# Hash logits of 14 heads in two products per half, compared in PSUM, in a fused LSH attention and MoE kernel

## The chip, the cores and the metric

One NeuronCore of a Trainium2 chip runs the whole kernel in one launch. The metric is device time in microseconds (us); lower is better. Matrix products run on TensorE (PE in the profile, its weight loads PEld), elementwise work on VectorE (DVE), ScalarE (ACT) and GpSimd (POOL), and SyncE (SP) issues nearly all DMAs.

## What is computed

Three stages in a row, all in float32 at the interface:

```python
q_bits = (einsum('bhsd,dk->bhsk', q, proj) > 0)      # 2 batches, 8 heads, 768 tokens, 64 channels, 6 bits
k_bits = (einsum('bhsd,dk->bhsk', k, proj) > 0)
mask   = bucket(q_bits)[..., :, None] == bucket(k_bits)[..., None, :]
scores = where(mask, q @ k.T / 8, -1e9)
x      = softmax(scores) @ v                         # -> 1536 x 512
x      = gelu_sigmoid(x @ w_in) @ w_out              # 512 -> 2048 -> 512
x      = mish(x @ w2_in) @ w2_out                    # 512 -> 2048 -> 512
```

The products run in a reduced format (fp32r), so each operand is split into a high part (the rounded value) and a low part (the remainder), and a product is the sum of high x high, low x high and high x low.

## The kernel before, in words

Attention takes the first 230 us or so. Its 16 heads are 96 steps of 128 queries (`NSTEP`), six steps to a head. In a step, PE computes one block of scores (`qk`, line 613: two products of `kh` with `qx`, two of `kb` with `qb`, 384 columns each), transposes two blocks of earlier probabilities (`trp`, line 676, six products), and multiplies earlier probabilities with the values (`pv`, lines 700 and 701). DVE takes the row minimum while it moves the scores to SBUF (`clamp`, line 625), ACT takes the exponential (`expo`, line 638). The transposed blocks are rounded by ACT (`pth`, line 683) and their remainder is taken by DVE (`ptl`, line 688). The order of a step is a string, `ORDER = "ACaBbETQPR"`: A and B are the two transposes with ACT's rounding, C the clamp, a and b DVE's remainders, E the exponential, T whatever a table of due steps (`todo`) holds for this step, Q the scores of the next step, P and R the products with the values. Every engine and every DMA queue works strictly in the order in which this loop issues. Transposes work on groups of three steps: a step whose number is a multiple of three opens a group, and its first transposes need the exponential of the step just before.

A head's operands are prepared about one head ahead by `prep(n)`. For head n, with b = 6(n-2), GpSimd starts at step b+2 (`start_prep`, function `s0` and `s1`): it scales and rounds q (high q goes into `qk_m`, and a DMA moves it to the lower half of `qx`), makes low q, copies `kh` (k is stored twice, in both halves of the partitions) and makes low k in `qk_m`. At step b+8 `s2` computes the hash logits in PE, six products of 384 columns (for either half of the tokens: `qk_m`, `kh` and `qx` against the projection matrix `pwt`), into one PSUM bank `prep`; right behind it DVE compares with 0 and scales into mask rows `mk`. Four DMAs (`s5`) copy rows of `mk` into `qb` and `kb`, where they add a large penalty to the scores of unequal buckets; `s4` (step b+5) moves low k and high q into the other rows of `qb` and `kb`, and `s3` (step b+6) splits the values (`vv`). For head 2 the steps are fixed: start at step 5, logits at 8, mask DMAs at 9; head 3 starts at step 8. The scores of head n are first needed at Q of step b+11.

GpSimd also merges the heads' outputs (`x_out`, `x_split`), and near the end of attention makes operands of the first MoE stage: `x_ops` (lines 301 to 315, L109), the weight sums `sf` (`ssums`, lines 277 to 283) and a weight split (L261). ACT rounds the sums (`sh`, line 291) at step 89. Every one of these has its due step in `todo`. After attention the MoE stages run 500 us of products with PE never idle for long.

Of the kernel before, what the change touches and what calls it, by code (L numbers as in the profile page):

```python
# [30 lines left out]
def mask_consts():  # L31
    c = np.zeros((64, 2), np.float32)
    c[12:18, 0] = -3.0e38
    c[0:18, 1] = 1.0
    c[38:44, 0] = -3.0e38
    c[32:38, 1] = -2.0 * CBIG
    c[38:50, 1] = CBIG
    return np.concatenate([c, c])
# [3 lines left out]
def lsh_attention_moe_kernel(  # L42
# [10 lines left out]
    B, H, D, S = qt.shape  # L53
    NTOK, DM = out.shape
# [56 lines left out]
    def rnd(ap):  # L111
        return ap.bitcast(F32)
# [238 lines left out]
    def attention():  # L351
        with ExitStack() as es:
# [18 lines left out]
            def load_q(n):  # L371
                b, h = head(n)
                t = nat.tile([P, S], F32, tag="qn", name="qn")
                if n == 0:
                    for f in range(2):
                        c = slice(f * HS, (f + 1) * HS)
                        nc.sync.dma_start(t[0:D, c], qt[b, h, 0:D, c])
                else:
                    nc.sync.dma_start(t[0:D], qt[b, h])
                nat_t["q", n] = t  # L380
# [63 lines left out]
            def pcol(j, o):  # L444
                w = pw[:, j, o : o + 2 * NB * (2 if o else 1)]
                return w.rearrange("p (a b) -> p a b", a=2)[:, :, 0:NB]

            def prep_w():
# [6 lines left out]
                nc.scalar.mul(pcol(0, 0), rnd(pr), -1.0)  # L455

            opnd = {}

            def prep(n):
# [41 lines left out]
                def s2():  # L501
                    pt = ps_t.tile([P, 512], F32, tag="pt", name="prep")
                    logits(pt, 0, 64, True, False)
                    logits(pt, 1, 0, False, True)
                    mk_box.append(pt)
# [11 lines left out]
                def s4():  # L517
                    nc.sync.dma_start(rnd(qb[D:P]), rnd(qk_m[0:D]))
                    nc.sync.dma_start(rnd(kb[D:P]), rnd(qk_m[D:P]))

                def s5():
                    mk = mk_box.pop()
                    for f in range(2):
                        c = slice(f * HS, (f + 1) * HS)
                        rows = (qb, f * D), (kb, f * D + 32)
                        for t, r in rows[::-1] if f else rows:
                            nc.sync.dma_start(rnd(t[0:32, c]), mk[r : r + 32])
# [62 lines left out]
                return s0, s1, s2, s3, s4, s5  # L590
# [166 lines left out]
            todo = {}  # L757

# [7 lines left out]
            at(1, zero_rows)  # L766

# [53 lines left out]
            for i in range(NSTEP + PVLAG):  # L821
# [14 lines left out]
                for op in ORDER if i != 2 else ORDER.replace("TQ", "QT"):  # L836
# [402 lines left out]
def layouts(q, k, v, proj, moe_w_in, moe_w_out, moe2_w_in, moe2_w_out):  # L1239
# [3 lines left out]
    qt = q.transpose(0, 1, 3, 2)  # L1243
# [44 lines left out]
```

## Time and profile before

| | |
|---|---|
| device time, 3 runs | 734.85, 732.07, 731.7 us (median 732.07) |
| the profiled execution | 733.5 us, of which 731.7 us is the span of the trace |
| PE busy | 724.4 us (99% of the span), 3856 products |
| DVE, ACT, POOL busy | 615.7, 468.5, 185.4 us |
| the chain that ended last | PE 91%, DVE 3%, ACT 3% of the span |
| lines of the chain | MoE output products (947) 35%, scores (613) 9%, transposes (676) 8%, values (700, 701) 8%, hash logits (493) 2% |
| granted TensorE clock | 1.0 of full speed throughout (2.4 GHz) |

Busy shares are means over stages. Up to about 225 us (attention) GpSimd is busy most of the time and then never again; PE is busy all the time in both. A time in the rows below is from the start of the span; a bracket behind a row tells how long the engine sat idle before it and what ended the wait.

### The profile page before, as it was taken

Reading aid. Unit: us, or ns where it says so; the run is one execution under the profiler, and the core shown is the slowest. Engines: PE = TensorE matmul, PEld = TensorE weight load, DVE = VectorE, ACT = ScalarE, POOL = GpSimd, SP = SyncE. Lnnn points to the kernel's source line nnn. Section 1 sums busy time; section 2 is a strip of 40 time slices with the busy share of each in tenths; the row PEclk is TensorE's granted clock in tenths of the full one; section 3 lists DMA queues with packets and bytes.
Section 4 is the critical chain, followed back from the end, with each engine's and each line's share of the span. In section 5 each row is a group of like instructions: output and inputs, shape, how many; then the busy total and the mean of one; then the engine's idle time right before and its main releaser. Section 6 shows DMA issues by size and latency. Waiting matters only on the chain.

```text
span 731.7 us, 11140 instructions
## 1 busy us (share of the span) xinstructions
PE 724.4 (99%) x3856; PEld 631.5 (86%) x3856; DVE 615.7 (84%) x1134; ACT 468.5 (64%) x956; POOL 185.4 (25%) x188
## 2 busy tenths in 40 slices
PE   8999999999999999999999999999999999999998
PEld 5999999999998688888888888888888888888886
DVE  8888889989988859888878797998699899897864
ACT  7888888888898765536546465676635556455340
POOL 7958877878893000000000000000000000000000
PEclk9999999999999999999999999999999999999999
DMA  5745655656624311122211221301302222211004
GB/s 151 199 130 142 192 154 148 182 151 163 165 85 129 98 59 59 57 70 76 86 58 58 87 86 59 116 0 59 108 8 76 69 70 74 87 58 58 1 1 172
DMA packets 25992, 69.53 MB, mean 95 GB/s; under 512 B 4464, under 2 KB 6992, under 8 KB 25936
## 3 DMA queue, kind: packets, MB, share of 16 engines
q1 hardware_dynamic: 25632, 68.62, 31.9%
q8 instruction: 30, 0.49, 0.3%
q10 hardware_dynamic: 304, 0.20, 0.1%
q14 instruction: 26, 0.21, 0.1%
HBM read 49.09 MB, written 3.19 MB: 71 GB/s over the span
## 4 chain that ended last, share of the span: by engine, by line
PE 91%; DVE 3%; ACT 3%; DMA 1%; issue 1%; SPq 0%; POOL 0%; DVEq 0%; ACTq 0%
PE y L947 35%; PE X L1010 11%; PE s L613 9%; PE pt L676 8%; PE Y L1010 8%; PE W L1010 7%; PE u L701 4%; PE u L700 4%; PE h L346 2%; PE prep L493 2%; DMA rb<-scr 1%; ACT p L638 1%; ACT pth L683 1%; DVE wb L243 0%; DMA qn<-in_qt_dram 0%
## 5 line engine op out<-in xcount | busy, mean ns | idle before, releaser
L688 DVE TENSOR_TENSOR ptl<-pt,pth 128x384 fp32r<-128x384 f32 x192 | 98.1, 552 | 23.3 <-ACT pth L683 20.9
L683 ACT CAST pth<-pt 128x384 fp32r<-128x384 f32 x192 | 82.8, 484 | 29.6 <-PE pt L676 29.6
L638 ACT ACTIVATE p<-p,mn 128x768 f32<-128x768 f32 x96 | 91.2, 950 | 1.7 <-DVE p L625 1.4
L625 DVE TENSOR_SCALAR_CACHE_REDUCE p<-s 128x768 f32<-128x768 f32 x96 | 90.6, 945 | 1.1 <-PE s L613 1.1
L961 DVE TENSOR_TENSOR xq<-xq,y 128x512 f32<-128x512 f32 (+1 forms) x113 | 75.6, 679 | 13.8 <-PE y L947 13.0
L676 PE MATMUL pt<-ident,p 128*128 128x128 f32 x576 | 81.0, 274 | 0.1
L947 PE MATMUL y<-wh,gh 128*128 128x512 f32 (+1 forms) x194 | 75.4, 389 | 0.0
L947 PE MATMUL y<-wl,gh 128*128 128x512 f32 (+1 forms) x194 | 75.4, 389 | 0.0
L947 PE MATMUL y<-wh,gl 128*128 128x512 f32 (+1 forms) x194 | 75.2, 387 | 0.0
L947 PE MATMUL y<-gh,wh 128*128 128x512 f32 x192 | 75.1, 391 | 0.0
L947 PE MATMUL y<-gh,wl 128*128 128x512 f32 x192 | 74.9, 390 | 0.0
L947 PE MATMUL y<-gl,wh 128*128 128x512 f32 x192 | 74.7, 389 | 0.0
L259 ACT CAST wh<-wb 128x512 fp32r<-128x512 f32 x64 | 39.4, 619 | 54.6 <-DVE wb L246 26.2
L676 PEld LDWEIGHTS pt<-ident,p 128*128 128x128 f32 x576 | 68.5, 140 | 6.5 <-ACT p L638 2.4
L700 PE MATMUL u<-pth,vv 128*128 128x384 f32 x192 | 64.7, 337 | 0.0
L701 PE MATMUL u<-ptl,vv 128*128 128x384 f32 x192 | 64.5, 336 | 0.0
L613 PE MATMUL s<-kh,qx 128*128 128x384 f32 x192 | 55.6, 370 | 0.3 <-DVE p L625 0.3
L613 PE MATMUL s<-kb,qb 128*128 128x384 f32 x192 | 49.2, 337 | 1.1 <-POOL kb L109 0.9
L261 DVE TENSOR_TENSOR wl<-wb,wh 128x512 fp32r<-128x512 f32 x62 | 42.3, 687 | 3.9 <-ACT wh L259 3.6
L961 DVE TENSOR_TENSOR yr<-yr,y 128x512 f32<-128x512 f32 x56 | 38.2, 684 | 7.8 <-PE y L947 6.9
L947 PEld LDWEIGHTS y<-wh,gl 128*128 128x128 f32 x194 | 36.4, 188 | 7.6
L947 PEld LDWEIGHTS y<-gl,wh 128*128 128x128 f32 x192 | 36.0, 188 | 7.8
(271 smaller groups left out, 1841.6 us busy)
## 6 DMA issues: line engine op xcount, KB each, us to landing
raw<-in_wt_dram SPq DMA_DIRECT2D x64, 512.0 KB, 3.4
kn<-in_kt_dram SPq DMA_DIRECT2D x15, 384.0 KB, 5.0
vn<-in_vt_dram SPq DMA_DIRECT2D x8, 384.0 KB, 6.5
ul<-uh SPq DMA_DIRECT2D x16, 192.0 KB
rb<-scr SPq DMA_DIRECT2D x16, 192.0 KB, 3.6
qn<-in_qt_dram SPq DMA_DIRECT2D x15, 192.0 KB, 3.4
qx<-qk_m SPq DMA_DIRECT2D x15, 192.0 KB, 3.9
qb<-qk_m SPq DMA_DIRECT2D x15, 192.0 KB, 5.4
```

The lines of the kernel that those rows point to most:

```text
L261: sub(lo, wf, rnd(hi))
L613: nc.tensor.matmul(s[:, f, :HS], a[:, c], bb[:, f * HS : (f + 1) * HS], start=st, stop=not st,)
L625: nc.vector.tensor_scalar(sb, s[:, :, :HS], NEG, None, ALU.min, ALU.min, accum_out=mn)
L638: nc.scalar.activation(p, p, AF.Exp, bias=mn, scale=-1.0, accum_out=z_t[u][:, zc : zc + 1],)
L676: nc.tensor.transpose(ptile[:, j * P : (j + 1) * P], p_t[3 * g + j][:, t * P : (t + 1) * P], ident,)
L683: nc.scalar.copy(hi, ptile[:, :HS])
L688: nc.vector.tensor_sub(lo, ptile[:, :HS], rnd(hi))
L700: nc.tensor.matmul(ut[:, :HS], vv[:, t, :], hi, start=(t == 0), stop=False)
L701: nc.tensor.matmul(ut[:, :HS], vv[:, t, :], lo, start=False, stop=(t == NT - 1))
L947: nc.tensor.matmul(y, w[:, js] if m == 0 else x[:, js], x if m == 0 else w[:, i0:i1], start=(n == 0), stop=(n == 5),)
L961: nc.vector.tensor_add(acc, acc, y)
L1010: nc.tensor.matmul(bk[b], w[:, k], x, start=(first and i == 0), stop=(hook is not None and i == 2), skip_group_check=True,)
```

## The change

Heads 2 to 15 no longer use `pwt` with three operands but one 128-column matrix `px` with two operands, `qx` (low q above, high q below) and `qk_m` (high k above, low k below), so that a half takes two products, four in all. The high and the low products land in different rows of the PSUM bank: ACT copies the rows 64 to 127, negated, into `mk`, DVE compares the rows 0 to 63 with them (`is_gt`), and GpSimd multiplies the 32 rows that belong to `kb` by a constant. For this q is loaded twice, as k already was (128 partitions, 384 KB), GpSimd makes `kh` first and all of `qx` in one scaling, and the DMA that moved high q into `qx` is replaced by one (`s6`) that moves high k into `qk_m`. The steps are: start b+2, `s6` b+3, logits and ACT's copy b+7, compare and multiply at C of step b+8 (`mid`), mask DMAs at T of b+8. For head 2: start 5, `s6` 5, logits 8, compare 9, mask DMAs 9. `px` is filled once, at steps 1 and 4: a memset, three small copies and two small DMAs. The mask rows that are copied are 12 of 32.

```diff
     D //= 2
-                    nc.sync.dma_start(t[0:D], qt[b, h])
+                    nc.sync.dma_start(t, qt[b, h])
...
             def zero_rows():
...
+                nc.gpsimd.memset(rnd(px), 0.0)
...
+            def prep_x():
+                o = 32 + NB
+                q, k, ql, kl = (slice(x, x + 2 * NB) for x in (12, 44, 76, 108))
+                pcopy(px[:, 0, q], rnd(pw[:, 0, 0 : 2 * NB]))
+                pcopy(px[0:D, 1, k], rnd(pw[0:D, 1, o : o + 2 * NB]))
+                pcopy(px[D:P, 1, k], rnd(pw[D:P, 2, o : o + 2 * NB]))
+                nc.sync.dma_start(rnd(px[D:P, 0, ql]), rnd(pw[0:D, 2, 0 : 2 * NB]))
+                nc.sync.dma_start(rnd(px[0:D, 1, kl]), rnd(pw[D:P, 1, o : o + 2 * NB]))
...
                 def s0():
+                    if n > 1:
+                        pcopy(kh, kn)
+                        nc.gpsimd.tensor_scalar(qx, qn, QSCALE, 1.0, ALU.mult, ALU.mult)
+                        nc.gpsimd.tensor_scalar(qn[0:D], qn[0:D], QSCALE, 1.0, ALU.mult, ALU.mult)
+                        nc.gpsimd.tensor_sub(qx[0:D], qn[0:D], rnd(qx[0:D]))
+                        return
                     nc.gpsimd.tensor_scalar(qk_m[0:D], qn[0:D], QSCALE, 1.0, ALU.mult, ALU.mult)
                     nc.sync.dma_start(rnd(qx[D:P]), rnd(qk_m[0:D]))
-                    if n > 1:
-                        nc.gpsimd.tensor_scalar(qn[0:D], qn[0:D], QSCALE, 1.0, ALU.mult, ALU.mult)
-                        nc.gpsimd.tensor_sub(qx[0:D], qn[0:D], rnd(qk_m[0:D]))
 
                 def s1():
-                    pcopy(kh, kn)
                     nc.gpsimd.tensor_sub(qk_m[D:P], kn[D:P], rnd(kh[D:P]))
...
                 def s2():
                     pt = ps_t.tile([P, 512], F32, tag="pt", name="prep")
+                    mk_box.append(pt)
+                    if n > 1:
+                        for f in range(2):
+                            for j, x in enumerate((qx, qk_m)):
+                                nc.tensor.matmul(
+                                    pt[:, :HS],
+                                    px[:, j, 12 - 12 * f : 140 - 12 * f],
+                                    x[:, f * HS : (f + 1) * HS],
+                                    start=(f + j == 0),
+                                    stop=(f + j == 2),
+                                )
+                        mk = hd.tile([P, HS], F32, tag="mk", name="mk", bufs=1)
+                        mk_box.append(mk)
+                        nc.scalar.mul(mk[0:64], pt[64:128, :HS], -1.0)
+                        return
...
+                def s2m():
                     if n > 1:
-                        s2m()
-
-                def s2m():
+                        pt, mk = mk_box
+                        del mk_box[0]
+                        nc.vector.tensor_tensor(mk[0:64], pt[0:64, :HS], mk[0:64], ALU.is_gt)
+                        nc.gpsimd.tensor_scalar(
+                            mk[32:64], mk[32:64], -2.0 * CBIG, 1.0, ALU.mult, ALU.mult
+                        )
+                        return
...
                 def s4():
-                    nc.sync.dma_start(rnd(qb[D:P]), rnd(qk_m[0:D]))
+                    nc.sync.dma_start(rnd(qb[D:P]), rnd(qx[D:P] if n > 1 else qk_m[0:D]))
...
+                def s6():
+                    nc.sync.dma_start(rnd(qk_m[0:D]), rnd(kh[0:D]))
...
-                for f, early, late in ((s2, 8, 8), (s3, 11, 6), (s4, 6, 5), (s5, 9, 9)):
+                for f, early, late in ((s6, 5, 3), (s2, 8, 7), (s3, 11, 6), (s4, 6, 5), (s5, 9, 8)):
                     at(early if n == 2 else b0 + late, f)
+                mid.setdefault(9 if n == 2 else b0 + 8, []).append(s2m)
...
                     elif op == "C" and i < NSTEP:
                         clamp(i)
+                        for f in mid.pop(i, ()):
+                            f()
```

How the instructions move, at three places. Line numbers in the rows are those of the kernel that a row is from; a number behind a name tells tiles of one name apart.

First place, PE in the steady cycle, at the logits of head 4 (`prep` the logits, `s` scores, `pt` transposes of the probabilities `p`). Before:

```order
L493 MATMUL prep_895<-qx_666,pwt_146 128x384
L613 MATMUL s_904<-kh_446,qx_447 128x384 x2
L613 MATMUL s_904<-kb1_142,qb1_140 128x384 x2
...
L676 MATMUL pt_913<-ident_123,p_806 128x128
L676 MATMUL pt_913<-ident_123,p_840 128x128
L676 MATMUL pt_913<-ident_123,p_873 128x128
```

After:

```order
L524 MATMUL prep_863<-qk_m_683,px_149 128x384
L655 MATMUL s_870<-kh_453,qx_454 128x384 x2
L655 MATMUL s_870<-kb1_142,qb1_140 128x384 x2
...
L718 MATMUL pt_880<-ident_123,p_709 128x128
L718 MATMUL pt_880<-ident_123,p_743 128x128
L718 MATMUL pt_880<-ident_123,p_777 128x128
...
L655 MATMUL s_914<-kh_453,qx_454 128x384 x2
L655 MATMUL s_914<-kb1_142,qb1_140 128x384 x2
...
L718 MATMUL pt_923<-ident_123,p_813 128x128
L718 MATMUL pt_923<-ident_123,p_847 128x128
L718 MATMUL pt_923<-ident_123,p_887 128x128
```

Before, the transposes after the logits' step open a new group; now a whole step with the last transposes of the old group (p_709 to p_777) stands between them.

Second place, GpSimd and SP around head 2 (`kb1`, `qb1` are zeroed rows of head 1's operands, `vv` the values). GpSimd before:

```order
L109 TENSOR_SCALAR qb1_140<-zero_137 32x768
L473 TENSOR_SCALAR qk_m_338<-qn_212 64x768
L476 TENSOR_SCALAR qn_212<-qn_212 64x768
L477 TENSOR_TENSOR qx_337<-qn_212,qk_m_338 64x768
L109 TENSOR_SCALAR kh_336<-kn_214 128x768
L481 TENSOR_TENSOR qk_m_338<-kn_214,kh_336 64x768
...
L473 TENSOR_SCALAR qk_m_448<-qn_374 64x768
...
L481 TENSOR_TENSOR qk_m_448<-kn_376,kh_446 64x768
L109 TENSOR_SCALAR vv_563<-vn_444 128x6x64
```

After:

```order
L111 TENSOR_SCALAR qb1_140<-zero_137 32x768
L437 MEMSET px_149 128x280
L111 TENSOR_SCALAR px_149<-pwt_146 128x12
L111 TENSOR_SCALAR px_149<-pwt_146 64x12 x2
L111 TENSOR_SCALAR kh_343<-kn_215 128x768
L490 TENSOR_SCALAR qx_344<-qn_213 128x768
...
L111 TENSOR_SCALAR kh_453<-kn_383 128x768
...
L498 TENSOR_TENSOR qk_m_455<-kn_383,kh_453 64x768
L543 TENSOR_SCALAR mk_466<-mk_466 32x384
L111 TENSOR_SCALAR vv_570<-vn_451 128x6x64
```

The multiply of head 2's mask (mk_466) stands behind all of head 3's preparation (kh_453 to qk_m_455), and `px` ahead of head 2's. SP there, after:

```order
L569 DMA qb0_139<-mk_466 12x384
L569 DMA kb0_141<-mk_466 12x384
L569 DMA kb0_141<-mk_466 12x384
L569 DMA qb0_139<-mk_466 12x384
L559 DMA qk_m_455<-kh_453 64x768
```

Head 3's move of high k into `qk_m` stands behind the mask DMAs of head 2.

Third place, GpSimd near the end of attention (`z` row sums, `sf` weight sums, `t2h` to `b21h` operands of the first MoE stage). Before:

```order
L650 TENSOR_SCALAR z_2818<-z_2818 128x12
L313 TENSOR_TENSOR xq_74<-xq_74 128x512 x2
L279 TENSOR_TENSOR sf_3239<-wb_1892,wb_2786 128x256
L109 TENSOR_SCALAR t2h_3344<-xq_74 128x512
L301 TENSOR_TENSOR t2l_3345<-xq_74,t2h_3344 128x512
L281 TENSOR_TENSOR sf_3239<-sf_3239,wb_1892 128x256
L315 TENSOR_TENSOR xq_74<-xq_74 128x512
L109 TENSOR_SCALAR b21h_3389<-xq_74 128x512
L283 TENSOR_TENSOR sf_3239<-wb_1892,sf_3239 128x256
```

After:

```order
L692 TENSOR_SCALAR z_2825<-z_2825 128x12
L315 TENSOR_TENSOR xq_74<-xq_74 128x512 x2
L281 TENSOR_TENSOR sf_3246<-wb_1899,wb_2793 128x256
L543 TENSOR_SCALAR mk_3326<-mk_3326 32x384
L111 TENSOR_SCALAR t2h_3360<-xq_74 128x512
L303 TENSOR_TENSOR t2l_3361<-xq_74,t2h_3360 128x512
L283 TENSOR_TENSOR sf_3246<-sf_3246,wb_1899 128x256
L317 TENSOR_TENSOR xq_74<-xq_74 128x512
L111 TENSOR_SCALAR b21h_3400<-xq_74 128x512
L285 TENSOR_TENSOR sf_3246<-wb_1899,sf_3246 128x256
```

The multiply of head 15's mask (mk_3326) stands in the middle of this work, ahead of the last sums.

## Rows read from the trace of the kernel before

**Rows 1.** The chain of waits, 60 to 100 us: by line, then one piece

```profile
by line: PE s L613 31.3%; PE pt L676 30.7%; PE u L701 15.3%; PE u L700 14.8%; PE prep L493 7.8%; PE prep L657 0.5%
...
65.09 1.04 PE prep L493 x6
```

**Rows 2.** Timeline, PE: start us, us, engine line op tile, idle before

```profile
80.89 0.81 PE L676 MATMUL pt<-ident,p 128*128 128x128 f32 x6
...
87.03 1.03 PE L676 MATMUL pt<-ident,p 128*128 128x128 f32 x6
```

**Rows 3.** Waits, all engines: total us, times, longest

```profile
PEld pt L676 <- ACT p L638: 2.4, 10, 0.3
```

**Rows 4.** Timeline, ACT, ahead of the transposes at 87.03 us

```profile
86.31 0.95 ACT L638 ACTIVATE p<-p,mn 128x768 f32<-128x768 f32 x1
```

**Rows 5.** Timeline, POOL, then PE, at the start

```profile
8.11 1.29 POOL L109 TENSOR_SCALAR kb<-qk_m 64x384 fp32r<-64x384 f32 x1
9.45 0.79 PE L613 MATMUL s<-kb,qb 128*128 128x384 f32 x3 [0.91 <-POOL kb L109]
```

**Rows 6.** Windows: us, busy of PE PEld DVE ACT POOL, PEclk, DMA share, GB/s

```profile
5.00:6.00 1.00, 0.75 (x5) 0.65 (x4) 0.94 (x3) 0.95 (x3) 0.54 (x1) 1.00 0.99 255
...
7.00:8.00 1.00, 0.98 (x6) 0.54 (x5) 1.00 (x2) 0.51 (x1) 0.92 (x2) 1.00 0.86 338
```

**Rows 7.** Timeline, POOL, up to head 3's preparation

```profile
1.25 0.47 POOL L438 MEMSET wzero<- 128x448 f32 x1
...
3.68 0.20 POOL L109 TENSOR_SCALAR pwt<-pr 64x12 fp32r<-64x12 f32 x1
...
15.16 0.82 POOL L473 TENSOR_SCALAR qk_m<-qn 64x768 fp32r<-64x768 f32 x1
...
29.69 0.51 POOL L109 TENSOR_SCALAR vv<-vn 128x384 fp32r<-128x384 f32 x1
```

**Rows 8.** Timeline, PE (head 2's first scores, step 13), SP (mask DMAs)

```profile
31.85 0.51 PE L613 MATMUL s<-kb,qb 128*128 128x384 f32 x2
...
35.73 0.59 PE L613 MATMUL s<-kh,qx 128*128 128x384 f32 x2
...
27.00 1.22 SPq L527 DMA_DIRECT2D kb<-mk  x2
```

**Rows 9.** The instructions of tile mk, then of qk_m: DMA issue to landing

```profile
DMA to landing us min/median/max: 1.9/2.0/3.8
...
DMA to landing us min/median/max: 3.9/4.8/5.4
```

**Rows 10.** Timeline, POOL, heads 14 and 15 and the sums

```profile
170.84 0.82 POOL L473 TENSOR_SCALAR qk_m<-qn 64x768 fp32r<-64x768 f32 x1 [1.73 <-DMA qn<-in_qt_dram]
...
193.78 0.74 POOL L731 TENSOR_TENSOR xq<-ul,rb 128x256 f32<-128x256 f32 x1 [1.11 <-DMA rb<-scr]
...
196.41 0.73 POOL L277 TENSOR_TENSOR sf<-wb 128x256 f32<-128x256 f32 x1 [0.63 <-DVE wb L243]
...
202.28 0.63 POOL L109 TENSOR_SCALAR t2h<-xq 128x512 fp32r<-128x512 f32 x1
...
206.76 0.74 POOL L283 TENSOR_TENSOR sf<-wb,sf 128x256 f32<-128x256 f32 x1
```

**Rows 11.** Timeline, PE (logits of heads 13, 15; scores of step 89), ACT

```profile
173.20 0.42 PE L493 MATMUL prep<-qk_m,pwt 128*128 128x384 f32 x1
...
200.42 0.42 PE L493 MATMUL prep<-qk_m,pwt 128*128 128x384 f32 x1
...
208.13 0.51 PE L613 MATMUL s<-kb,qb 128*128 128x384 f32 x2
...
209.43 1.05 ACT L291 CAST sh<-sf 128x1024 fp32r<-128x1024 f32 x1
```

**Rows 12.** The page's costliest groups: line engine op xcount | busy, mean ns

```profile
L688 DVE TENSOR_TENSOR ptl<-pt,pth 128x384 fp32r<-128x384 f32 x192 | 98.1, 552 | 23.3 <-ACT pth L683 20.9
...
L625 DVE TENSOR_SCALAR_CACHE_REDUCE p<-s 128x768 f32<-128x768 f32 x96 | 90.6, 945 | 1.1 <-PE s L613 1.1
```

More of the change, by code (lines that the diff above doesn't have):

```diff
@@ L33, in mask_consts @@
     c[12:18, 0] = -3.0e38
[L34 to L37, printed above, removed]
+    c[0:12, 1] = 1.0
+    c[12:18, 1] = -0.5
+    c[32:38, 0] = -3.0e38
+    c[32:38, 1] = CBIG
+    c[38:50, 1] = -2.0 * CBIG
     return np.concatenate([c, c])
@@ L53, in lsh_attention_moe_kernel @@
     B, H, D, S = qt.shape
+    D //= 2
     NTOK, DM = out.shape
@@ L444, in pcol @@
             def pcol(j, o):
-                w = pw[:, j, o : o + 2 * NB * (2 if o else 1)]
-                return w.rearrange("p (a b) -> p a b", a=2)[:, :, 0:NB]
+                o += NB if o else 0
+                return pw[:, j, o : o + 2 * NB].rearrange("p (a b) -> p a b", a=2)
             def prep_w():
@@ L455, in prep_w @@
                 nc.scalar.mul(pcol(0, 0), rnd(pr), -1.0)
+            px = wo[0].tile([P, DM], F32R, tag="ol1", name="px")[:, 0:280]
+            px = px.rearrange("p (a b) -> p a b", a=2)
+            def prep_x():
[6 more added lines that the diff above has]
+                nc.sync.dma_start(rnd(px[0:D, 1, kl]), rnd(pw[D:P, 1, o : o + 2 * NB]))
             opnd = {}
@@ L502, in s2 @@
                     pt = ps_t.tile([P, 512], F32, tag="pt", name="prep")
+                    mk_box.append(pt)
[13 more added lines that the diff above has]
+                        return
                     logits(pt, 0, 64, True, False)
                     logits(pt, 1, 0, False, True)
-                    mk_box.append(pt)
+                def s2m():
                     if n > 1:
-                        s2m()
-                def s2m():
+                        pt, mk = mk_box
[5 more added lines that the diff above has]
+                        return
                     pt = mk_box.pop()
@@ L524, in s5 @@
                         c = slice(f * HS, (f + 1) * HS)
-                        rows = (qb, f * D), (kb, f * D + 32)
-                        for t, r in rows[::-1] if f else rows:
-                            nc.sync.dma_start(rnd(t[0:32, c]), mk[r : r + 32])
+                        rows = (qb, f * D, 0, 32), (kb, f * D + 32, 0, 32)
+                        if n > 1:
+                            rows = (qb, f * 12, 0, 12), (kb, f * 12 + 32, 6, 12)
+                        for t, r, a, w in rows[::-1] if f else rows:
+                            nc.sync.dma_start(rnd(t[a : a + w, c]), mk[r : r + w])
                 def first(q1, k1):
@@ L589, in prep @@
                     return s0, lambda: nc.scalar.copy(kh, kn), second, s2, s3, s4, s5, s2m
-                return s0, s1, s2, s3, s4, s5
+                return s0, s1, s2, s3, s4, s5, s2m, s6
             NSTEP = NHD * NT
@@ L757, in attention @@
             todo = {}
+            mid = {}
             def at(step, f, *args):
@@ L766, in attention @@
             at(1, zero_rows)
+            at(4, prep_x)
             for f, st in zip(second[3:7], (2, 7, 1, 3)):
@@ L772, in start_prep @@
                 b0 = NT * (n - 2)
-                s0, s1, s2, s3, s4, s5 = prep(n)
+                s0, s1, s2, s3, s4, s5, s2m, s6 = prep(n)
                 s0()
                 s1()
-                for f, early, late in ((s2, 8, 8), (s3, 11, 6), (s4, 6, 5), (s5, 9, 9)):
+                for f, early, late in ((s6, 5, 3), (s2, 8, 7), (s3, 11, 6), (s4, 6, 5), (s5, 9, 8)):
                     at(early if n == 2 else b0 + late, f)
+                mid.setdefault(9 if n == 2 else b0 + 8, []).append(s2m)
             for u in range(NHD // 2 - 1):
@@ L1242, in layouts @@
     NB = proj.shape[1]
-    qt = q.transpose(0, 1, 3, 2)
+    qt = np.concatenate([q.transpose(0, 1, 3, 2)] * 2, axis=2)
     kt = np.concatenate([k.transpose(0, 1, 3, 2)] * 2, axis=2)
```

## The prediction

> **What bounds the kernel now.** I read the chain of waits first: between 60 and 100 us every piece of it is PE, the hash logits with 7.8% among them [rows 1]. So in attention PE sets the pace, a product that goes saves its own time, and a wait in front of PE costs its whole length. Next, the PE timeline against the table of waits: six transposes normally take 0.81 us by the trace, but 1.03 us where they open a group of three steps [rows 2], and the table names the reason: PE waits for ACT's exponential, 10 times, 2.4 us in all [rows 3]. The ACT timeline shows how close that is: the exponential ends at 86.31 + 0.95 = 87.26 us, the transposes that need it began at 87.03 [rows 4]. The reader should see that a plain step, (87.03 - 80.89) / 3 = 2.05 us [rows 2], is 0.22 us too short for transposes, two roundings and an exponential. Last, GpSimd's own timeline, at the start and the end of attention, where it has no gap [rows 7, 10].
>
> **Products removed.** Six logits take 1.04 us [rows 1], 0.173 each. Two fewer for 14 heads: 28 x 0.173 = 4.86 us saved, all on PE. The two other products only change operands.
>
> **Logits one step earlier.** Before, the logits' step precedes a step that opens a group: its extra 1.04 us covers ACT, and the transposes at 80.89 show no wait, while half a head later, at 87.03, they lose 0.22 [rows 2]. The order shows that from head 3 on a plain step comes between. Then both openings in a head follow plain steps, and both lose 0.22: 13 heads (3 to 15) x 0.22 = 2.86 us given back. The bounds are 0 and 0.3 each [rows 3]; I take 0.22 because it is the same sequence on the same engines.
>
> **ACT's copy, DVE's compare.** The copy reads PSUM behind the logits while PE goes on with scores, ahead of ACT's next rounding; I cost it at nothing, and if ACT had no such gap it would enlarge the 0.22. The compare takes about 0.55 us, as DVE's remainder with one PSUM and one SBUF input does [rows 12], in place of a scaling of the same tile. Neither ends a wait of PE in the steady cycle.
>
> **GpSimd in the steady cycle.** One preparation has five instructions of the same sizes as before, and one multiply is new. I price it at 0.51 us, the copy of 384 columns in that cycle [rows 7]; the upper end is 1.29 us, a copy of 384 columns beside a busy DVE [rows 5]. The multiply waits for the compare, so the next preparation cannot start before it: GpSimd loses its lead. It had time to spare, since it waited for q's load before a preparation (1.73 us at head 14 [rows 10]). The load of k, which it now needs first, is issued four steps ahead, so 8 us. In SP's queue `s6` takes the place of another move. Cost nothing here.
>
> **Start.** Head 1's q has 384 KB instead of 192. GpSimd's scaling of it stands right before the copy of `kb` (8.11 us) for which PE waits 0.91 us [rows 5]. The bounds are 0 and 0.6 us (192 KB more at the 338 GB/s of [rows 6]); I take 0.3. With the 64 rows of q in flight the DMA engines were 0.99 busy for 255 GB/s, later 0.86 busy for 338 [rows 6]. The Trainium skill (SBUF — State Buffer, section Door 1: The DMA port swizzle) says that 64 rows reach only half of the 16 ports, so that 128 rows with twice the bytes would take no longer; by that the term is 0 and the sum 733.7. The two windows lean that way but mix several loads.
>
> **Head 2's mask.** GpSimd is without a gap from 15.16 us, head 2's preparation, to 29.69, the end of head 3's [rows 7]. In front of that come now the memset of `px` (280 columns, at most the 0.47 of 448; I take 0.35) and three copies of 0.20 with gaps of 0.08 [rows 7]: 1.2 us, with the start's 0.3 it makes 1.5. The multiply stands behind head 3's preparation: it starts at 29.69 + 1.5 = 31.19 and ends at 31.74. The second `kb` DMA is issued 0.61 later (half of 1.22 [rows 8]) and lands 2.0 after that [rows 9]: 34.35. PE wants it at 31.85 + 0.17 [rows 8], less 0.35 for head 2's products, plus 0.3: 31.97. PE waits 2.38; the 0.22 of the next opening falls into it, so 2.16. SP and all behind it wait too: head 3's `s6` is issued after two more mask issues, at 33.57, and lands 3.9 to 5.4 later [rows 9], at 37.5 to 39.0. Head 3's logits would come at 35.73 [rows 8] - 0.35 + 0.3 + 2.16 = 37.84, the first product with `qk_m` 0.17 later. A wait of 0 to 1.0, 0.4 at the median; I take 0.3.
>
> **Head 15's mask and the sums.** From head 14's preparation to the place of head 15's multiply GpSimd works 202.28 - 170.84 = 31.44 us, less 1.11 and 0.63 of waits [rows 10] whose cause will be done by then, plus two multiplies with gaps, 1.1: 30.8. PE needs from logits 13 to logits 15 only 200.42 - 173.20 = 27.22 [rows 11], less 2 x (0.35 - 0.22): 26.96. So the multiply starts 3.84 us behind its compare. The compare ends 0.69 (logits) + 0.69 (scores) + 0.95 + 0.55 [rows 12] = 2.88 us after the logits begin. The mask is wanted 208.13 + 0.17 - 200.42 = 7.88 us after them [rows 11], with a step more and the two changes above 7.88 + 2.05 + 0.22 - 0.35 = 9.80, so 6.92 behind the compare; it is there at 3.84 + 0.55 + 0.61 + 2.0 = 7.0. A wait of 0.1, just at the edge (0 to 2.3 by the price of the multiply). The weight sums end 206.76 + 0.74 - 202.28 = 5.22 after the multiply [rows 10], 2.88 + 3.84 + 0.55 + 5.22 = 12.49 behind the logits. ACT's rounding `sh` was due 209.43 - 200.42 = 9.01 behind them [rows 11], now 9.01 + 2.05 + 0.22 - 0.35 + 0.1 = 11.03. ACT stands still for 1.46 us, with the roundings of the transposes queued behind. PE gets most of it one step later; between 0 and 1.46 I take 1.1.
>
> **Sum.** -4.86 + 2.86 + 0.3 + 2.16 + 0.3 + 0.1 + 1.1 = +1.96 us. The profiled execution took 733.5 us, the median of the runs is 732.07; the MoE stages are shifted, not changed, so the median moves to **734.0**. A measurement here can tell about 0.5%, 3.66 us, from no change: 728.4 to 735.7.
>
> **Rivals.** (1) *The queues have slack after all*: ACT and GpSimd are in time and only products and start count: 732.07 - 4.86 + 0.3 = 727.5. It needs head 2's multiply to end by 31.97 - 2.0 - 0.61 = 29.36, 2.4 us sooner than its queue allows; the gapless GpSimd of [rows 7] speaks against. (2) *The second opening of a group does not wait*, because ACT happens to be ahead there: 734.0 - 2.86 = 731.1. For it: the price is a near miss of 0.22 us. Against: [rows 2 to 4], always the same distance. (3) *Slower: the multiply is dear.* If a multiply takes 1.29 us [rows 5], head 2's mask is 0.78 later, head 15's three multiplies (13, 14, 15) 2.3 later, all straight into PE's wait: 734.0 + 0.78 + 2.3 = 737.1. The result leaves the 0.5% where the four together cost 1.7 us more, a multiply of about 0.95 us. [...] That some stall lies elsewhere at the end, where the sums are late for ACT, leads to the same side.
>
> **Chances.** Forecast 0.50 (its own ends: 732.2 with the start, `s6`, the edge and `sh` at nothing, 735.4 with all at their upper bounds but the multiply), rival 2 0.14, rival 1 0.11, rival 3 0.25. So faster 0.11, within 0.5% 0.64, slower 0.25. The range 730.5 to 737.8 takes in the forecast, rivals 2 and 3 and leaves out rival 1 and the tails.
>
> **What would show it.** Right: 28 products fewer; the table of waits has PE waiting for ACT's exponential some 23 times instead of 10; PE waits over 2 us for a `kb` DMA near 32 us and some tenths at the logits of head 3; GpSimd runs head 3's preparation ahead of head 2's multiply; ACT waits over 1 us for `sf` near 211 us; PE in the MoE stages is as before. Wrong: no wait of PE near 32 us, or openings of a group that take 0.81 us everywhere (rivals 1 and 2); a multiply near 1 us, and a mask wait of 2 us near 208 us (rival 3).

## The result and the profile after

The changed kernel took 742.51 us (median of 4 runs, 741.78 to 743.23), the kernel before 732.51 on the same chip: ratio 1.0136, 95% interval 1.0121 to 1.0151. It is 10 us slower, where +2 was forecast and 737.8 was the upper end of the range. The profiled execution has a span of 741.4 us, 9.7 more than before. Page of the changed kernel, engines and chain:

```profile
PE 727.1 (98%) x3828; PEld 630.5 (85%) x3828; DVE 619.6 (84%) x1134; ACT 475.8 (64%) x970; POOL 194.3 (26%) x206
...
PE 87%; ACT 4%; DVE 3%; DMA 3%; issue 1%; POOL 1%; SPq 0%; DVEq 0%; POOLq 0%; ACTq 0%
```

PE has its 28 products fewer (3828 in place of 3856), and yet the end is later. Its waits, in the same view as [rows 3] (total us, times, longest):

```profile
POOL mk L543 <- DVE mk L542: 18.7, 4, 8.4
...
PEld pt L718 <- ACT p L680: 5.8, 23, 0.5
...
PE s L655 <- issue: 3.9, 1, 3.9
...
POOL kh L111 <- DMA kn<-in_kt_dram: 2.2, 1, 2.2
...
PE s L655 <- DMA qb<-mk: 1.1, 1, 1.1
```

PE waits 23 times for the exponential, as forecast, in place of the 10 of [rows 3]. New are one stop of 3.9 us (for "issue" the trace names nothing that ended it), a wait of GpSimd for k, a late mask row (`qb<-mk`), and GpSimd standing before its multiply (`mk`). To see where the 9.7 us arise, take DVE's clamp, one for each of the 96 steps, and subtract its start before from its start after. This is worked out from the two DVE timelines (us). Each row is one profiled execution, and executions of one kernel differ (the change 741.78 to 743.23 us, the multiply on DVE 732.6 to 740.0), so a difference between two rows counts only where waits in the traces bear it out:

| kernel | step 8 | step 16 | step 46 | step 83 | step 95 |
|---|---|---|---|---|---|
| the change | 0.12 | 6.35 | 5.83 | 7.58 | 11.11 |
| head 3 prepared behind the multiply | 0.15 | -0.30 | -0.80 | 0.91 | 4.07 |
| stop filled with products | 0.20 | 3.79 | 3.29 | 4.96 | 8.17 |
| q of 64 rows | -0.20 | 4.69 | 4.18 | 6.00 | 9.17 |
| multiply on DVE | -0.01 | -0.41 | -0.66 | 1.69 | 3.09 |
| before, logits one step earlier | 0.17 | 0.39 | 1.56 | 3.80 | 4.40 |
| multiply on DVE, logits one step later | 0.00 | -0.34 | -1.59 | 0.82 | 5.30 |
| head 3 behind, conversions later | 0.14 | -0.28 | -0.78 | -0.16 | 2.63 |
| multiply on DVE, k first | 0.00 | 0.30 | 1.04 | 1.30 | 2.37 |
| multiply from PSUM | -0.02 | 0.86 | 2.29 | 3.52 | 4.23 |
| head 3 behind, conversions later, sums first | 0.06 | -0.39 | -0.90 | -0.77 | 0.05 |

The change loses 6.2 us at head 2 (up to step 16), wins 0.5 in the five heads up to step 46, loses 1.75 up to step 83 and 3.5 at the end of attention; 1.4 come back behind it (9.7 of 11.1 are left in the span). PE of the kernel before waited in the first MoE stage for operands from DVE:

```profile
247.68 0.50 PE L1010 MATMUL X<-t2l,sh 128*128 128x512 f32 x1 [0.92 <-DVE t2l L301]
250.21 0.50 PE L1010 MATMUL X<-t3h,sh 128*128 128x512 f32 x1 [0.42 <-DVE q L1031]
```

In the changed kernel 0.2 us of this is left. The other rows of the table are the experiments.

**Head 2.** Timelines of the changed kernel, GpSimd, SP and PE (start us, us, idle before):

```profile
23.45 1.02 POOL L624 TENSOR_TENSOR vv<-vn,vv 128x384 fp32r<-128x384 f32 x1
26.63 0.83 POOL L111 TENSOR_SCALAR kh<-kn 128x768 fp32r<-128x768 f32 x1 [2.16 <-DMA kn<-in_kt_dram]
...
31.17 1.82 POOL L498 TENSOR_TENSOR qk_m<-kn,kh 64x768 fp32r<-64x768 f32 x1
33.08 0.50 POOL L543 TENSOR_SCALAR mk<-mk 32x384 f32<-32x384 f32 x1
...
33.60 1.53 SPq L569 DMA_DIRECT2D kb<-mk  x2
...
31.22 0.59 PE L655 MATMUL s<-kh,qx 128*128 128x384 f32 x2
35.75 1.42 PE L655 MATMUL s<-kb,qb 128*128 128x384 f32 x2 [3.94 <-issue]
...
38.24 1.48 PE L718 MATMUL pt<-ident,p 128*128 128x128 f32 x6
```

The chain is the forecast one, but GpSimd has a gap of 2.16 us ahead of head 3's preparation where the kernel before had none [rows 7]: it waits for k, whose load stands behind the larger q (run 3 tests how much of it that is). That PE's stop is for the mask is shown by run 1, where it goes with the late multiply. The multiply ends at 33.58, not at 31.74. Then the last row: six transposes take 1.48 us, not the 0.81 of [rows 2]. Windows of the changed kernel (us, busy of PE PEld DVE ACT POOL, PEclk, DMA share, GB/s):

```profile
33.00:34.00 1.00, 0.00 (x0) 0.00 (x0) 0.00 (x0) 0.01 (x1) 0.84 (x2) 1.00 0.00 0
34.00:35.00 1.00, 0.00 (x0) 0.00 (x0) 0.00 (x0) 0.00 (x0) 0.92 (x2) 0.62 0.00 2
...
36.00:38.00 2.00, 1.93 (x6) 1.53 (x7) 0.80 (x1) 0.00 (x0) 1.00 (x2) 0.50 0.50 105
...
41.00:42.00 1.00, 1.00 (x9) 0.97 (x8) 0.96 (x2) 0.39 (x3) 0.00 (x0) 0.96 1.06 313
```

The granted clock fell to 0.50, 1.2 GHz, while PE stood, and PE then worked for 5 us at half speed before 2.4 GHz came back.

### The profile page after: what moved, and what is told of

It reads as the page before. It is cut to its first block, busy times and chain, and to the rows that moved or that the text cites. A ratio compares the mean times of both kernels' runs of the same rounds, so it can differ in the third digit from the quotient of the medians.

```text
span 741.4 us, 11201 instructions
## 1 busy us (share of the span) xinstructions
PE 727.1 (98%) x3828; PEld 630.5 (85%) x3828; DVE 619.6 (84%) x1134; ACT 475.8 (64%) x970; POOL 194.3 (26%) x206
## 4 chain that ended last, share of the span: by engine, by line
PE 87%; ACT 4%; DVE 3%; DMA 3%; issue 1%; POOL 1%; SPq 0%; DVEq 0%; POOLq 0%; ACTq 0%
PE y L994 35%; PE X L1057 11%; PE pt L718 8%; PE Y L1057 7%; PE W L1057 7%; PE s L655 7%; PE u L742 4%; PE u L743 4%; PE h L348 3%; ACT p L680 1%; ACT pth L725 1%; PE prep L524 1%; DMA kn<-in_kt_dram 1%; DMA rb<-scr 1%; DMA kb<-mk 1%
## 5 line engine op out<-in xcount | busy, mean ns | idle before, releaser
L718 PE MATMUL pt<-ident,p 128*128 128x128 f32 x576 | 85.5, 278 | 1.5 <-DVE ptl L730 0.9
L655 PE MATMUL s<-kb,qb 128*128 128x384 f32 x192 | 51.1, 345 | 7.0 <-issue 3.9
L655 PEld LDWEIGHTS s<-kb,qb 128*128 128x128 f32 x192 | 35.4, 192 | 8.7 <-issue 4.2
```

Source lines behind the costliest of these rows:

```text
L655: nc.tensor.matmul(s[:, f, :HS], a[:, c], bb[:, f * HS : (f + 1) * HS], start=st, stop=not st,)
L718: nc.tensor.transpose(ptile[:, j * P : (j + 1) * P], p_t[3 * g + j][:, t * P : (t + 1) * P], ident,)
```

## The experiments

Ratios are to the kernel before on the same chip, with 95% intervals.

**1. Head 3's preparation behind the multiply.**

```diff
-                return 5 if n == 2 else NT * (n - 2) + 2
+                return {2: 5, 3: 9}.get(n, NT * (n - 2) + 2)
```

> The change, with GpSimd's preparation of head 3 issued four steps later (step 9), behind the multiply of head 2's mask, which now is first in GpSimd's queue; all else as in the change. Theory (queue): head 2's k mask was late only because its multiply stood behind a preparation that itself waited 2.16 us for head 3's k. Then PE's stop of 3.94 us near 32 us goes, and with it the stretch at 1.2 GHz behind it (some 2.6 us more): 742.5 - 3.9 - 2.6 = 736.0 us. Rival (transfer): the mask's 12-row transfers are slow by themselves; then a stop of over 2 us stays and the time is 740 us or more.

736.65 us, 1.0047 (1.0032 to 1.0063), and no stop near 32 us: the shift at step 16 is -0.30 in place of 6.35. So one misplaced instruction of 0.50 us cost 6.65 us. The rival falls.

**2. The stop filled with products of constants.**

```diff
-                        qk(i + 1, (0, 1) if i else (1,))
+                        if i == 11:
+                            qk(12, (0,))
+                            keep_warm(16, 512)
+                        qk(i + 1, (0, 1) if i and i != 11 else (1,))
```

> The change, with 16 products of constants (bf16, 512 columns, into a buffer nobody reads) issued between the k-high and the mask products of step 12, that is within PE's stop near 32 us. Theory (clock): the stop stays as long, but PE is busy in it, the granted clock stays at 2.4 GHz, and the slow rows behind it go: 742.5 - 2.6 = 739.9 us. Rival: the products behind the stop are slow because their operands come late; then the time is 742.5 us.

741.38 us, 1.0115 (1.0096 to 1.0135). Windows of this kernel, the stop and behind it:

```profile
31.00:35.00 4.00, 3.94 (x21) 2.08 (x21) 1.68 (x4) 1.82 (x5) 3.75 (x5) 1.00 0.02 5
35.00:38.00 3.00, 2.69 (x16) 2.14 (x15) 0.96 (x2) 0.47 (x2) 1.45 (x3) 1.00 0.51 126
```

PE is busy in the stop and the clock stays at 1.00. By the table the shift at step 16 is 3.79 in place of 6.35: the clock's share of head 2 is 2.56 us, the stop's 4.1. Shown in the traces; the ratios of 1.0136 and 1.0115 have intervals that just overlap (1.0121 and 1.0135).

**3. q of 64 rows from head 3 on**, so that the other 64 rows of these heads hold what an earlier head left.

```diff
+            q_keep = {}
...
-                t = nat.tile([P, S], F32, tag="qn", name="qn")
+                t = q_keep[n % 2] if n > 2 else nat.tile([P, S], F32, tag="qn", name="qn")
+                q_keep[n % 2] = t
...
-                    nc.sync.dma_start(t, qt[b, h])
+                    w = P if n < 3 else D
+                    nc.sync.dma_start(t[0:w], qt[b, h, 0:w])
```

> The change, with q of heads 3 to 15 loaded as 64 rows as before; the other 64 rows keep what an earlier head left there, so that the products of these heads are not the reference's. GpSimd does the same work. Theory (bytes): the doubled load is what holds head 3's k back (by about 1.1 us of the 2.16) and what holds the write of the softmax sums in its queue at head 14 (SP's wait for it 4.3 us before, 7.0 after). Then PE's stop near 32 us falls from 3.9 to about 2.8, SP's wait near 195 us falls to about 4.3, the stop at head 14 goes with its slow clock (-1.8 - 1.3): 742.5 - 1.1 - 3.1 = 738.3 us. Rival (queue alone): 742.5 us, both stops as in the change.

742.44 us, 1.0124 (1.0107 to 1.0141): not the 738 expected. GpSimd's wait for k falls, as the timeline of this kernel has it:

```profile
25.48 0.83 POOL L111 TENSOR_SCALAR kh<-kn 128x768 fp32r<-128x768 f32 x1 [0.93 <-DMA kn<-in_kt_dram]
```

PE's stop falls with it to 3.12 us, and the doubled load is 1.2 us of GpSimd's 2.16. But the loss behind step 83 is 3.17 us, much as with 128 rows. It is made up otherwise: the stop at head 14 is gone and the clock stays at 1.00, but the mask of head 15 now holds PE for 0.66 us and ACT waits 2.2 us for `sf`. SP's wait ahead of the sums' read falls to 5.8 us, not to 4.3; it is 5.4 and 5.7 in runs 1 and 2, which load 128 rows, so the doubled load is not what made it 7.0 in the change. What did stays open. The prediction drew on the Trainium skill (SBUF — State Buffer, section Door 1: The DMA port swizzle), by which 64 rows reach half of the 16 ports, and estimated from it that 128 rows with twice the bytes take no longer. Here the load behind them did come later (26.63 against 25.48 us). At the start, where this was weighed, +0.12 us was measured, between 0 and the 0.3 taken.

**4. The kernel before with its logits one step earlier.**

```diff
-((s2, 8, 8), (s3, 11, 6), (s4, 6, 5), (s5, 9, 9))
+((s2, 8, 7), (s3, 11, 6), (s4, 6, 5), (s5, 9, 9))
```

> The kernel before, with nothing changed but the step at which the hash logits of heads 3 to 15 and DVE's comparison are issued: one step earlier, as in the change. Theory (second opening): PE then waits 0.22 us for ACT's exponential a second time in each head, as it does in the change, 13 x 0.22 = +2.9 us, so 736 us beside 733.3. Rival: the second wait belongs to the new form of the logits, not to their step; then 733.3 us, and the 10 waits of before.

736.45 us, 1.0052 (1.0032 to 1.0072). Its table of waits:

```profile
PEld pt L676 <- ACT p L638: 6.3, 23, 1.2
```

23 waits, and (1.56 - 0.39) / 5 = 0.23 us a head. So the second opening comes with the earlier step and does not need the new form of the logits.

**5. The change with the multiply on DVE.**

```diff
-                        nc.gpsimd.tensor_scalar(
+                        nc.vector.tensor_scalar(
                             mk[32:64], mk[32:64], -2.0 * CBIG, 1.0, ALU.mult, ALU.mult
```

> The change, with the multiply of the mask's lower 32 rows on DVE, right behind DVE's comparison, not on GpSimd. Theory (queue): head 2's stop and its slow clock go as with the later preparation (-6.5). GpSimd also no longer sits waiting for a comparison ahead of every preparation, so that x_out's additions move earlier by about 2 us and no longer meet DVE's weight conversions at steps 47 and 59, which took 1.55 and 2.10 us where 0.42 and 0.69 is usual: -2.1 more, 733.9 us. Rival: the two conversions are slow for another reason; then 736. The stop at head 14 (1.8 us) stays in both, since SP stands behind the reciprocal's transfer there, not behind GpSimd.

735.82 us, 1.0038 (1.0017 to 1.006), but with a spread of 732.6 to 740.0 in 10 runs. Head 2's stop is gone, the loss at the end falls to 1.4 us. The conversions did not recover: 1.98 and 1.31 us in this kernel. The order of the queue was not the whole reason; see runs 7 and 8.

**6. The same with the logits one step later**, where they were before.

```diff
-((s6, 5, 3), (s2, 8, 7), (s3, 11, 6), (s4, 6, 5), (s5, 9, 8))
+((s6, 5, 3), (s2, 8, 8), (s3, 11, 6), (s4, 6, 5), (s5, 9, 9))
-                mid.setdefault(9 if n == 2 else b0 + 8, []).append(s2m)
+                mid.setdefault(9 if n == 2 else b0 + 9, []).append(s2m)
```

> The change with the multiply on DVE, and with the logits, the comparison and the issue of the mask rows of heads 3 to 15 moved back by one step, where they were before. Theory (second opening): the 0.22 us waits fall from 23 back to about 10, so 2.9 us less than with the multiply on DVE alone: 735.8 - 2.9 = 732.9 us. Rival: the mask now lands too late for the head's first step, PE waits for it and the gain is lost: 735 us or more.

739.41 us, 1.0095 (1.0066 to 1.0123). Both came true. Up to step 46 it wins (1.59 - 0.34) / 5 = 0.25 us a head, 0.20 more than run 5, and the waits fall back:

```profile
PEld pt L718 <- ACT p L680: 2.9, 12, 0.4
...
113.48 0.58 PE L655 MATMUL s<-kb,qb 128*128 128x384 f32 x2 [2.29 <-DMA kb<-mk]
...
197.96 0.41 PE L655 MATMUL s<-kb,qb 128*128 128x384 f32 x1 [2.86 <-DMA qb<-mk]
```

But at heads 8 and 14 the mask comes late and takes it all: SP stands 6.0 and 6.9 us before its read of the softmax sums (`rb`), the mask rows queued behind. Behind the stop at head 14 the clock was at 0.50 from 199 to 201 us; behind the 2.29 us at head 8 it stayed at 1.00. So the earlier step buys time for the mask and pays with the second opening.

**7. Conversions later.** Why does the change lose 1.75 us between steps 46 and 83? Timelines of the changed kernel, GpSimd and DVE, at the two jumps, then the same DVE instructions before:

```profile
119.65 1.83 POOL L767 TENSOR_TENSOR ul<-ul,uh 128x768 f32<-128x768 f32 x1
...
120.23 1.55 DVE L240 TENSOR_SCALAR raw<-raw 128x512 uint32<-128x512 uint32 x1
...
147.48 1.83 POOL L767 TENSOR_TENSOR ul<-ul,uh 128x768 f32<-128x768 f32 x1
...
147.76 2.10 DVE L245 SCALAR_TENSOR_TENSOR wb<-wb,raw 128x512 uint32<-128x512 uint32 x1
```

```profile
114.08 0.42 DVE L238 TENSOR_SCALAR raw<-raw 128x512 uint32<-128x512 uint32 x1
...
141.21 0.72 DVE L243 SCALAR_TENSOR_TENSOR wb<-wb,raw 128x512 uint32<-128x512 uint32 x1
```

DVE's conversion of a weight ends 0.3 and 0.5 us behind GpSimd's addition. GpSimd, tied to PE by its multiply, now runs these additions about 5 us later against PE (119.65 - 108.71 less PE's shift of 5.84), just there. The edit moves the conversions, on top of run 1:

```diff
-    WOF = ((-1, -1, 11, 14, 18), (-1, 1, 11, 13, 17))
+    WOF = ((-1, 1, 13, 14, 18), (-1, 1, 11, 13, 17))
```

> The change with head 3's preparation behind the multiply, and with DVE's two weight conversions of steps 47 and 59 issued two steps later, where GpSimd by the trace sits idle. Theory (shared reads): DVE's conversion of 32-bit integers (0.42 and 0.69 us alone) stands until GpSimd's running instruction with two inputs has ended (1.58 and 2.08 us in that kernel), and PE waits for DVE behind it. Moved, both take their short time and the shift at these steps, 0.7 and 1.2 us, goes: 736.65 - 1.9 = 734.7 us. Rival: the conversions are long by what stands in them, or in the transfer of the weights; then they stay over 1.5 us wherever they run, and the time stays at 736.6.

735.69 us, 1.0044 (1.0031 to 1.0058), by the medians not to be told from run 1. They take 0.90 and 1.45 us now, beside a shorter instruction of GpSimd with two inputs, and the table shows 1.1 us won at step 83. Each again ends 0.3 and 0.5 us behind that instruction. Their length goes with what GpSimd runs, so the rival falls; the gain was about half of what was expected.

**8. The multiply read from PSUM.**

```diff
-                        nc.vector.tensor_tensor(mk[0:64], pt[0:64, :HS], mk[0:64], ALU.is_gt)
-                        nc.gpsimd.tensor_scalar(
-                            mk[32:64], mk[32:64], -2.0 * CBIG, 1.0, ALU.mult, ALU.mult
+                        a, b = slice(0, 32), slice(32, 64)
+                        nc.vector.tensor_tensor(pt[b, :HS], pt[b, :HS], mk[b], ALU.is_gt)
+                        nc.vector.tensor_tensor(mk[a], pt[a, :HS], mk[a], ALU.is_gt)
+                        nc.vector.tensor_scalar(
+                            mk[b], pt[b, :HS], -2.0 * CBIG, 1.0, ALU.mult, ALU.mult
                         )
```

> The change with the multiply on DVE, but read from PSUM: the comparison of the lower 32 rows is left in PSUM and the multiply takes it from there (three DVE instructions in place of two). Theory (shared reads): DVE's multiply that read and wrote only SBUF was held by GpSimd's two-input instructions like the weight conversions (1.82 us in place of 0.48 at one head), while DVE's instructions that read PSUM are not; so no multiply takes over 0.6 us, the jumps at those heads go, the spread of the runs narrows, 735.8 - 1.0 = 734.8 us. Rival: it is not the read but the queue; then single multiplies stay over 1 us and the time stays at 735.8.

737.86 us, 1.0088 (1.0072 to 1.0105). The multiply in run 5, then here (ns min/median/max):

```profile
L543 DVE TENSOR_SCALAR mk<-mk x14: 350/505/1886, 27.4 to 203.8; 32x384 f32<-32x384 f32 x14
```

```profile
L545 DVE TENSOR_SCALAR mk<-prep x14: 550/550/551, 28.1 to 206.2; 32x384 f32<-32x384 f32 x14
```

From SBUF to SBUF it takes 0.35 to 1.89 us, 1.89 beside a subtraction of GpSimd with two inputs; from PSUM always 0.55, also at 206.24, beside an instruction of GpSimd with two inputs. So it is the read of SBUF that is held. The rival, the queue alone, falls; the forecast time was missed by 3 us all the same. The gain is lost to the third instruction: DVE is 0.3 us a head late, by the table (2.29 - 0.86) / 5.

**9. k loaded ahead of q**, on top of run 5 (the two load lines change places).

> The change with the multiply on DVE, and k of each head loaded ahead of its q, since GpSimd's preparation begins with k. Theory: with the multiply gone from GpSimd its preparations wait for k's transfer instead (1 to 6.5 us, each head), which comes behind q's doubled one; k first lets GpSimd run some 1 us earlier at each head, its additions no longer meet the conversions, and the loss at the last steps (1.4 us) shrinks: 735.8 - 1.5 = 734.3 us, with a smaller spread. Rival: the preparation only waits for q instead, one instruction later; 735.8 us.

734.84 us, 1.0029 (1.0015 to 1.0042), against 1.0038 with q first: the intervals overlap, so nothing is shown of the time. The multiply's median is 970 ns here, since GpSimd meets DVE elsewhere. One row shows more, GpSimd's and DVE's timelines at head 2:

```profile
27.30 0.83 POOL L491 TENSOR_SCALAR qn<-qn 64x768 f32<-64x768 f32 x1
27.39 0.95 DVE L543 TENSOR_SCALAR mk<-mk 32x384 f32<-32x384 f32 x1
```

GpSimd's instruction has a single input here, and DVE's still ends only 0.2 us behind it. So one with two inputs holds DVE longer because it runs longer (1.84 us), and not by a rule of its own.

**10. The last sums first in GpSimd's queue**, on top of run 7.

```diff
-    XOP = ((4, 1.22), (2, 0.56), (1, 0.41))
+    XOP = ((4, 1.22), (4, 0.56), (1, 0.41))
```

In run 1 the end of attention looks otherwise than in the change: no late mask at head 14, 0.59 us at head 15, and ACT waits for GpSimd (timelines of run 1, PE and ACT):

```profile
210.38 0.41 PE L655 MATMUL s<-kb,qb 128*128 128x384 f32 x1 [0.32 <-DMA kb<-mk]
211.06 0.44 PE L655 MATMUL s<-kb,qb 128*128 128x384 f32 x1 [0.27 <-DMA kb<-mk]
...
213.47 1.05 ACT L293 CAST sh<-sf 128x1024 fp32r<-128x1024 f32 x1 [2.19 <-POOL sf L285]
```

In the change itself ACT does not wait there; it is the mask of head 14, behind SP's wait for the sums, and then the clock (of the change: a row of ACT, SP's table of waits from 150 to 222 us, rows of SP and PE, and a window):

```profile
220.54 1.04 ACT L293 CAST sh<-sf 128x1024 fp32r<-128x1024 f32 x1
...
SPq L711 <- DMA scr<-zt: 11.4, 2, 7.0
...
198.69 1.11 SPq L711 DMA_DIRECT2D rb<-scr  x2
199.89 1.12 SPq L569 DMA_DIRECT2D qb<-mk  x1
...
203.25 0.41 PE L655 MATMUL s<-kb,qb 128*128 128x384 f32 x1 [1.13 <-DMA qb<-mk]
204.33 0.44 PE L655 MATMUL s<-kb,qb 128*128 128x384 f32 x1 [0.66 <-DMA kb<-mk]
...
205.00:208.00 3.00, 3.00 (x13) 2.90 (x12) 1.63 (x4) 1.29 (x3) 2.92 (x3) 0.50 0.95 258
```

The two stops make 1.79 of the 3.53 us that the change loses from step 83 to 95. The other 1.7 fit the second stretch at 1.2 GHz, which no run isolates. In runs 1, 3 and 2 the same steps lose 3.16, 3.17 and 3.21 us with no such stretch, and with head 15's mask and ACT's wait in its place.

> The change with head 3's preparation behind the multiply and the two conversions later (735.7 us so far), and with the second set of GpSimd's splits and differences of x (t2, b21, t3 and on) issued two steps later, so that the sums sf of the last weights stand ahead of them in GpSimd's queue. Theory (GpSimd late at the end): the 2.6 us that are lost behind step 83 come from ACT's wait of 2.16 us for sf; with it gone 735.7 - 2.4 = 733.3 us. Rival: PE is held there by something else of GpSimd (head 15's mask, x_out); then ACT's wait goes and the time stays within 0.5 us of 735.7.

734.73 us, 1.0032 (1.002 to 1.0043). By the ratios it is not to be told from run 7 (1.0031 to 1.0058); by the traces it is. The loss behind step 83 is 0.8 us in place of 2.8, both waits are gone, and the clamp of step 95 is at +0.05 us. So in the kernel of run 7 it was GpSimd, late with head 15's mask and with `sf`. That the same holds for the change is not shown, since its loss took the other path. The other 1.2 us of this kernel's span (732.9) arise behind step 95; a weight conversion beside GpSimd takes 1.66 us there, at 229.53, but the kernel before has one of 1.65 at 224.69, so their cause stays open.

**11. Several at once.** Six more kernels joined the edits above. All were slower than the kernel before, and all missed their forecast. First the multiply from PSUM, k first, conversions later:

> The same with k loaded ahead of q and the two conversions of steps 47 and 59 two steps later. Theory: 734.8, less 1 us each for the two: 732.8 us, level with the kernel before. Rival: GpSimd is set by the transfers of k and q and meets DVE at other steps; 734 us or more.

738.41 us, 1.0093 (1.0078 to 1.0108): the rival's side. With the logits one step later at 10 heads:

> The last one, with the logits, the comparison and the mask's issue one step later (where they were before) for all heads from the third on but 8, 11 and 14, at which SP's queue stands behind the write of the softmax sums. Theory: 10 second openings less, 10 x 0.22 = -2.2: 730.6 us, faster than the kernel before. Rival: the mask lands late at some of these heads too; 732 us or more.

743.1 us, 1.0158 (1.0143 to 1.0174). A mask was late (1.5 us), and the second openings did not go:

```profile
PEld pt L720 <- ACT p L682: 9.4, 26, 0.8
```

With the multiply read from PSUM the step alone does not decide on them, as it did in runs 4 and 6. At all heads, with SP's read of the sums later:

> The same with the logits one step later at all heads from the fourth on, and with SP's issue of the reciprocals' reads for the first six pairs three steps later, so that the mask rows no longer stand behind it. Theory (SP's queue): no stop of PE at heads 8 and 14, all 13 second openings gone: 732.8 - 2.9 = 729.9 us. Rival: the sums now come late for GpSimd's products, or the masks late by their own chain (comparison, multiply, four issues of 0.76 us); stops of over 1 us remain and the time is 732 us or more.

753.63 us, 1.0301 (1.0279 to 1.0323): the sums come late for GpSimd, DVE waits for GpSimd's `z`, and PE waits 7 times for mask rows of `kb`. The openings stay here too (27). Run 10 with the logits of 9 heads two steps earlier:

> The same, with heads 4 to 12 having their logits and comparison two steps earlier yet (and their preparation and loads one step earlier, k ahead of q). Theory: whether the logits open a second wait for ACT's exponential depends on their place in the cycle of three steps in which ACT also copies u; two steps earlier is three steps before the old place, so the second waits go at 9 heads, 9 x 0.22 = -2.0: 731.3 us, about 14 waits in all. Rival: any place but the old one opens the second wait; 23 waits and 733.3 us. Second rival: the preparation is not done in time, PE stands at the logits and the time is above 734.

751.93 us, 1.0271 (1.025 to 1.0292); the second rival: PE stands at the logits, up to 2.1 us. Why only the old step opens no second wait stays open. The last two:

> The change with the multiply on DVE, the two conversions two steps later, the last sums first in GpSimd's queue, and the logits one step later (where they were before) for all heads from the third on but 8, 11 and 14. Theory: each cause shown so far is taken away where it is cheap; 735.8 - 1.0 (conversions) - 1.0 (sums) - 10 x 0.22 (second openings) = 731.6 us, within 0.5% of the kernel before. Rival: what is gained at the openings is lost again to GpSimd's holding of DVE's multiply and to late masks; 734 us or more.

738.37 us, 1.0089 (1.0064 to 1.0114): 12 openings, but masks late at heads 4, 8, 12 and 14, up to 1.8 us.

> The last of the GpSimd versions (head 3 behind the multiply, conversions later, last sums first; 734.7 us) with the logits one step later for heads 3 to 7, 9, 10 and 12, the multiply still on GpSimd and the next head's preparation behind it, one step later too. Theory: 8 second openings less, no multiply of DVE to be held: 734.7 - 8 x 0.22 = 732.9 us. Rival: the masks land late, since the multiply now starts a step later and the transfers take as long as before; stops of PE for the mask rows appear and the time is 735 us or more.

751.21 us, 1.0262 (1.0239 to 1.0284): the logits wait for the move of `kh`, up to 5.6 us. The gains do not add up: where these kernels save an opening, a mask or a preparation comes late.

## Why the prediction was wrong

- **Products removed, logits one step earlier**: right. 28 products and 23 waits as forecast; 0.23 us a head by run 4 for a second opening (0.22 taken). Together they won 0.10 us a head (5.83 against 6.35 over five), where 0.35 - 0.22 = 0.13 was forecast.
- **Head 2's mask**: the chain was right, the size not. Forecast 2.16 + 0.3, measured 6.65. The step "GpSimd is without a gap" failed: it waited 2.16 us for head 3's k, whose load was not followed through SP's queue behind the doubled q. Each mask issue took SP 0.77 us, not 0.61. And the sum has no term for the clock, since "a wait in front of PE costs its whole length": 2.56 us by run 2. The 0.3 for head 3's logits did not come; PE starts them without a wait, at 42.20 us.
- **GpSimd in the steady cycle, "Cost nothing here"**: failed. The text said that GpSimd loses its lead and asked only whether its own work stays in time. What it meets later was not asked: its additions moved onto DVE's conversions, some 2.4 us (1.75 and the 0.6 that six heads should have won). Run 7 took 1.1 of them back; that the rest has the same cause is argued from the rows.
- **Head 15's mask and the sums**: failed in the change, 1.2 us forecast against 3.5. The loss came by a path without a term: at head 14 the mask rows stood in SP's queue behind the read of the sums, for which SP stood 7.0 us (4.3 before), two stops of PE made 1.79 us, and about 1.7 more went with the second stretch at 1.2 GHz. The two forecast waits are not in the change. They are in run 1, PE for head 15's mask 0.59 us (0.1 forecast) and ACT for `sf` 2.19 us (1.46 forecast), and run 10 shows that GpSimd's lateness makes them. The text also called GpSimd gapless at the end, where [rows 10] show waits of 1.11 and 0.63 us.
- **Start**: 0.12 for 0.3. **The MoE stages** were not only shifted: 1.4 us came back there, where PE had waited before.
- **The rivals**: all three are out. There was no slack (rival 1), the second openings do wait (rival 2), and the multiply is not dear (rival 3): it takes 0.50 us on GpSimd at all 14 heads, as taken. The result lies above the range for reasons that none of them names.

The terms by the table: -0.30 (start, products of heads 2 and 3) + 6.65 - 0.52 + 1.75 + 3.53 - 1.4 = 9.7 us. The forecast had the right sign, but it priced each wait by its length alone, without the clock, and followed neither SP's queue nor what a later GpSimd meets.

## What to carry to other kernels

An instruction that waits for PE's results, put into a queue that until then ran ahead of PE, ties the whole queue to PE: price what stands behind it and whom the delayed work now meets, not the instruction. A stop of PE of some 4 us cost 2.6 us more by the clock than its length. Taking one wait away can bring up the next: in runs 1 to 3 the stop at head 14 was gone or halved, the waits for head 15's mask and the sums came up, and the loss stayed near 3.2 us until run 10 mended the queue that made them late.

## What the runs showed of the hardware

- DVE and GpSimd: DVE's instructions that take all inputs from SBUF (conversions 0.42 and 0.72 us, the multiply 0.35) were held to 1.55, 2.10 and 1.89 us, until 0.2 to 0.6 us behind the end of GpSimd's running instruction. One input was enough on GpSimd's side (0.95 us in run 9), and two held longer as they ran longer. The multiply that read PSUM kept its 0.55 at all 14 heads. The Trainium skill (SBUF — State Buffer, section Who interferes with whom) tells of a port pair that the two share, as an exclusive lock. Runs 8 and 9 agree.
- The clock: after PE had stood for 3.9 us it worked at 1.2 GHz for about 5 us, 2.56 us lost; filled with products of constants, the same stop left it at 2.4 GHz. Two stops of 1.13 and 0.66 us with one product between were also followed by 1.2 GHz (about 3 us), one of 2.29 us in run 6 was not.
- SP mostly takes 0.71 to 0.80 us to issue a mask move of 12 rows (1.53 for two), 0.54 to 0.61 for one of 32 (1.22 for two [rows 8]).
